# One GpSimd multiplication for keys and receptances, and solve products of the second half in place with 128 columns, in a chunked recurrence with two MLPs

## The chip, the cores and the metric

The kernel runs on one core of one Trainium2 chip. The metric is the device time of one execution in microseconds (us); shorter is better. Engines are called TensorE (PE, with PEld for its weight loads), VectorE (DVE), ScalarE (ACT), GpSimd (POOL) and SyncE (SP). The clock that the profile lists is the one granted to TensorE, as a share of its full speed.

## The reference

For 4 batches and 8 heads, a state of 40 x 40 per head is carried over 768 steps; its outputs then go through two MLPs, token by token.

```
for t in range(S):                      # S = 768, D = 40, B = 4, H = 8
    y[:, :, t] = einsum('bhd,bhde->bhe', r_t, state)
    Sa = einsum('bhde,bhe->bhd', state, a_t)
    state = state * w_t[:, :, None, :] - einsum('bhd,bhe->bhde', Sa, b_t)
    state = state + einsum('bhd,bhe->bhde', v_t, k_t)
x = y by tokens                         # 3072 tokens x 320
h = x @ moe_w_in                        # 320 -> 2048
g = where(h >= 1, h, where(h <= -1, 0, (h + 1) ** 2 / 4))
x = g @ moe_w_out                       # 2048 -> 320
gate = x @ moe2_w_gate ; val = x @ moe2_w_val      # 320 -> 1536 each
out = (silu(gate) * val) @ moe2_w_out   # 1536 -> 320
```

## The kernel before

The sequence is cut into 12 chunks of 64 steps. A chunk of one batch with its 8 heads is a unit, so there are 48 units, numbered chunk by chunk. Within a chunk the recurrence becomes matrix products and one triangular solve; from chunk to chunk only the state is carried. Values that need more than 16 bits are held as a high and a low f16 part, and products are made of the parts.

Work comes in five kinds. `decay_tasks` (three groups of four chunks) multiplies the decays up, on VectorE for the first group and on GpSimd for the others, and writes them to DRAM as `was` and `wks`. `p_tasks` prepares a unit: it loads keys and receptances of two units at a time into the tile `ldp` and multiplies them by the decays. `ldp` has four parts of 128 rows: 0 holds k and b, 1 holds a and r, 2 and 3 hold the decays that they are multiplied by (`wks` in both halves of the rows of part 2, of which the lower is a copy, and `was` in rows 0 to 63 of part 3). In part 1 only a is multiplied by decays (rows 0 to 63, the helper `mul`, L573, on VectorE for chunk 0 and GpSimd for the others); r (rows 64 to 127) is multiplied by 2^8 by the helper `scaled` (L576, GpSimd). Casts on ScalarE (L864, L868) and subtractions (L567) then make the f16 parts, two transposes follow, and products (L885) give the matrices of the unit.

`inv_tasks` inverts the triangular matrices of a chunk's 32 heads, in halves of 32 steps, on VectorE (62 operations in a row, L948 and L953), and stores the result to DRAM, from where `m_tasks` loads it as `tt`. `m_tasks` runs the recurrence of a unit: products into the PSUM tile `px` (L1065), then the solve in two halves of 32 steps. Each half reads its 32 rows of `px`, makes three f16 parts (`xs`) of them, and multiplies by `tt` in 8 products, one per head (`mm_sa`, L1075), that write 32 other rows of `px` (64 to 95, 96 to 127); from these `shi` (L1106) and `slo` make the f16 parts of `vss`. Between the halves 16 products (L1081) subtract the first half from the second. Then follow the products that give the output and the next state (L1142, L1163).

The MLPs run chunk by chunk: `in1` and `in2` with the input products (L1208), `outp` with the output products (L1275), on the PSUM tiles `ph` and `po`. In the beginning PSUM and SBUF lend their tiles to other uses: `po` is at first used for the recurrence of chunk 0 under the name `pq`, and is given to `outp` when the tasks named in `K.grow("po", ...)` have ended. Weights are split into f16 parts by VectorE, ScalarE and GpSimd while the first chunks run.

The order of all instructions on each engine comes from the class `Plan`, which runs at build time. It simulates the engines with the costs given with each task, forward and backward by turns (`rounds`), and emits the tasks in the order of the last forward pass. `lim` bounds how far transfers may queue up ahead, a constant in `forward` and one in `backward` stand for the time to a landing, and the tables `by_chunk` and `by_step` add offsets to the priorities of named tasks: `K.nudge` in every round, `K.last` before the last. A task with `lk=True` may not overlap with one of the other of VectorE and GpSimd in the plan.

Of the kernel before, what the change touches and what calls it, by code (L numbers as in the profile page):

```python
# [15 lines left out]
class Plan:  # L16
# [10 lines left out]
    def __init__(self):  # L27
        self.tasks, self.made, self.pools, self.slots = [], {}, {}, {}
        self.bias, self.unit, self.nudge, self.last = 0.0, ["z", 0, 0], ({}, {}), ({}, {})
        self.lim, self.rounds, self.loose = 1.438, 5, ()  # L30

    def pool(self, name, tiles):
        self.pools[name] = dict(free=list(tiles), users={}, spares=[], grow=[])
# [35 lines left out]
    def forward(self, prio):  # L69
# [59 lines left out]
        while done < len(ts):  # L129
            started = True  # L130
            while started:
                started = False
                for eng in self.ENGINES[:5]:
# [7 lines left out]
                    while any(heaps):  # L141
# [42 lines left out]
                        if t["dma"]:  # L184
                            heapq.heappush(events, (end, -1))
                            dma = max(dma, begin) + t["dma"]
                            end = dma + 1.705
                        else:
                            end += t["lat"]
                        heapq.heappush(events, (end, i))  # L190
# [29 lines left out]
    def backward(self, prio):  # L220
# [14 lines left out]
        now, done, starts, held, events, size = 0.0, 0, [0.0] * len(ts), set(), [], len(ts)  # L235

        def lat(t):
            return 1.13 + t["dma"] if t["dma"] else t["lat"]

        seen = set()  # L240

# [104 lines left out]
def tile_recurrence__then__gated_mlps(  # L346
# [94 lines left out]
    sbt("ldv", [128, 2, H, D], F32, 1)  # L441
    sbt("vh", [128, H, D], F16, 2)
    sbt("xs", [128, H, D], F16, 2)
    sbt("tt", [128, 2, 2, H, HC], F16, 1)
    gfs = sbt("gf", [128, H, C], F32, 1)
    K.pool("sr", [gfs[0][0:D].bitcast(F16).rearrange("p h t -> p (h t)")[:, 0:3 * HD].rearrange(
        "p (l h d) -> p l h d", l=3, h=H)])
# [41 lines left out]
    K.spare("px", ph, first_m)  # L489
    K.pool("pq", po)  # L490
    K.grow("ph", ph, [(("m", n), "sl", 1) for n in range(B)])
    K.grow("po", [po], [(("m", n), x) for n in range(B) for x in ("s2", "xf")])
    late_keys = [("p", n) for n in range(2 * B, NSU)]
    next_keys = [("p", n) for n in range(B, 2 * B)]

# [76 lines left out]
    def mul(e, out, x, y):  # L572
        e.tensor_tensor(out=out, in0=x, in1=y, op=ALU.mult)  # L573

    def scaled(x, scale):
        p_.tensor_scalar(  # L576
            out=x, in0=x, scalar1=scale, scalar2=1.0, op0=ALU.mult, op1=ALU.mult)

    def side(pool, n):

        return (p_, "Pool", c_p(n)) if pool else (v_, "DVE", c_v(n))
# [1 line left out]
    def setup():  # L583
        v_.memset(mask, 2.0**-6)
        for h0 in (0, C):
            p_.affine_select(
                out=mask[h0:h0 + C], in_=mask[h0:h0 + C], pattern=[[1, C]],
                compare_op=ALU.is_gt, fill=0.0, base=0, channel_multiplier=-1,
            )
        p_.memset(eyem, 0.0)  # L590
        for g in range(2):
            p_.affine_select(
                out=eyem[64 * g:64 * g + 64], in_=eyem[64 * g:64 * g + 64],
                pattern=[[-2, 16], [1, HC]], compare_op=ALU.not_equal, fill=1.0, base=-g,
                channel_multiplier=0)
        p_.memset(sel, 0.0)
        for l in range(2):
            p_.affine_select(
                out=sel[:, 0:D], in_=sel[:, 0:D], pattern=[[-1, D]], compare_op=ALU.not_equal,
                fill=2.0**6, base=-D * l, channel_multiplier=1)  # L600
        p_.memset(eye16, 1.0)
        p_.affine_select(
            out=eye16, in_=eye16, pattern=[[1, 128]], compare_op=ALU.is_equal, fill=0.0, base=0,
            channel_multiplier=-1)
        for t in kbs + kbs2 + ars + vss + K.pools["ars"]["spares"][0][0]:
            v_.memset(t[:, :, 120:128], 0.0)
        for t in vss:
            v_.memset(t[64:128, :, 0:120], 0.0)
        v_.memset(ss[0][64:128], 0.0)
        v_.memset(wt[0][:, :, :, 104:128], 0.0)  # L610
        v_.memset(x16[0][:, 704:768], 0.0)

# [209 lines left out]
    def p_tasks(n, p):  # L822
# [24 lines left out]
        if j % 2 == 0:  # L847
# [6 lines left out]
            T(eng, cost, lambda: copy(  # L854
                out=G("ldp", pp)[C:128, 2], in_=G("ldp", pp)[0:C, 2]),
              r=[(pp, 4)], w=[(pp, 2)], use=L, p=p - 4)
            T("Pool", c_ps(2 * HD), lambda: scaled(G("ldp", pp)[C:128, 1], 2.0**8),
              r=[(pp, 1)], w=[(pp, 5)], use=L, p=p - 4)
        e0, eng, cost = side(c in ARP, HD)
        T(eng, cost, lk=True, emit=lambda: mul(e0, f(1)[0:C], f(1)[0:C], f(3)[0:C]),  # L860
          r=[(pp, 1), (pp, 3)] + (["pads"] if c < 2 else []), w=[(key, "ar")], use=L, p=p)
        T("Pool", c_p(HD), lambda: mul(p_, f(0), f(0), f(2)),
          r=[(pp, 0), (pp, 2)], w=[(key, "kb")], use=L, p=p)
        T("ACT", c_s(2 * HD), lambda: s_.activation(  # L864
            out=G("ars", key)[:, :, 0:2 * D].rearrange("p h (x d) -> p h x d", x=2),
            in_=two(f(1)), func=AF.Copy),
          r=[(key, "ar"), (pp, 5)], w=[(key, "arh")], use=L + AS, p=p)
        T("ACT", c_s(2 * HD), lambda: s_.activation(  # L868
            out=hi2(G("kbs", key)), in_=two(f(0)), func=AF.Copy),
          r=[(key, "kb")], w=[(key, "kbh")], use=L + KB_, p=p)  # L870
# [47 lines left out]
    def inv_tasks(c, p):  # L918
# [38 lines left out]
        for i0 in range(0, 2 * HC - 2, span):  # L957
            part = [divmod(i, 2) for i in range(i0, min(i0 + span, 2 * HC - 2))]

            def steps(part=part):  # L960
                for j, q in part:
                    step(j, q)

            T("DVE", sum(c_v((j // 2 + 1) * (HC - 1 - j)) for j, _ in part), steps,
              r=[(key, "j", i0)], w=[(key, "j", min(i0 + span, 2 * HC - 2))], use=ub + pm, p=p)
        T("ACT", c_s(512), lambda: s_.activation(
            out=T16()[:, 0], in_=M(), func=AF.Copy, scale=2.0**8),
          r=[(key, "j", 2 * HC - 2)], w=[(key, "h")], use=ub + pm, p=p)
        T("DVE", c_v(512), lambda: split(T16()[:, 1], M(), 2.0**8, T16()[:, 0]),
          r=[(key, "h")], w=[(key, "l")], use=ub + pm, p=p)  # L970

        for g in range(2):
# [32 lines left out]
    def m_tasks(n, p):  # L1005
# [15 lines left out]
        if j % 2 == 0:  # L1021
# [8 lines left out]
            if not last:  # L1030
# [2 lines left out]
                    in_=fdr[c][ps].unsqueeze(0).to_broadcast([D, 2 * H, D])),  # L1033
                    r=[("f", c)], w=[(mp, "f")], use=FF, p=p + 4, dma=0.36, cost=0.68)
            td = tsd[c][:, :, :, ps]
            DMA(lambda e: e.dma_start(
                out=G("tt", mp)[0:64].rearrange("p f j h t -> p f (j h t)"),
                in_=td.rearrange("l s f b t -> (l s) f (b t)")),
                r=[("tsd", c)], w=[(mp, "tt")], use=TT, p=p - 3, dma=0.5)
            DMA(lambda e: e.dma_start(  # L1040
                out=G("tt", mp)[64:96].rearrange("p f j h t -> p f (j h t)"),
                in_=td[0].rearrange("s f b t -> s f (b t)")),
                r=[("tsd", c)], w=[(mp, "tt")], use=TT, p=p - 3, dma=0.25, cost=0.68)

        T("ACT", c_s(HD), lambda: s_.activation(
# [23 lines left out]
          use=PX + LK + AT + VS + VH, p=p)  # L1069

        def mm_sa(hf):
            sa, tt, xs = hd(G("px", key)), G("tt", mp)[0:96, hf, j % 2], G("xs", (key, hf))[0:96]
            z = 64 + 32 * hf
            for h in range(H):
                t_.matmul(out=sa[z:z + 32, h], lhsT=tt[:, h], rhs=xs[:, h])  # L1075

        def mm_c():
            px, l2, vs = hd(G("px", key)), flat(G("l21", pk)), G("vss", key)
# [11 lines left out]
        def xhi(hf):  # L1090
            px, xs = hd(G("px", key)), G("xs", (key, hf))
            s_.activation(  # L1092
                out=xs[0:32], in_=px[32 * hf:32 * hf + 32], func=AF.Copy, scale=-(2.0**-10))

        def xdup(hf):
            xs = G("xs", (key, hf))
# [1 line left out]

        def xlo(hf):
            xs = G("xs", (key, hf))  # L1100
            split(xs[64:96], hd(G("px", key))[32 * hf:32 * hf + 32], -(2.0**-10),
                  xs[0:32])

        def shi(hf):
            z = slice(64 + 32 * hf, 96 + 32 * hf)
            s_.activation(out=hi2(G("vss", key)[z]), in_=two(hd(G("px", key))[z]),  # L1106
                          func=AF.Copy, scale=2.0**-8)

        def slo(hf):
            z = slice(64 + 32 * hf, 96 + 32 * hf)  # L1110
            vs = G("vss", key)
            split(vs[z, :, D:2 * D], hd(G("px", key))[z], 2.0**-8, vs[z, :, 0:D])

        for hf in range(2):
            T("ACT", c_s(HD), lambda hf=hf: xhi(hf), r=[(key, "x", hf)],
# [2 lines left out]
              w=[(key, "xl", hf)], use=XS[hf], p=p)  # L1118
            T("DVE", c_v(HD), lambda hf=hf: xlo(hf), r=[(key, "xh", hf)], w=[(key, "xl", hf)],
              use=PX + XS[hf], p=p)  # L1120
            T("PE", 0.39, lambda hf=hf: mm_sa(hf), r=[(key, "xl", hf), (mp, "tt")],
              w=[(key, "sa", hf)], use=PX + TT + XS[hf], p=p)
            T("ACT", c_s(2 * HD), lambda hf=hf: shi(hf), r=[(key, "sa", hf)],
              w=[(key, "sh", hf)], use=PX + VS, p=p)
# [190 lines left out]
    def by(tables):  # L1315
        return {(u, i): x for u, table in tables.items() for i, x in table.items()}

    by_chunk = by({
        "m": {40: -5.25},
        "p": {3: 0.02},  # L1320
    })
    by_step = by({
        "d": {84: 0.48},
    })
    K.nudge = by_chunk, by_step
    by_chunk = by({
# [9 lines left out]
    })  # L1336
    by_step = by({
# [10 lines left out]
    })  # L1348
    K.last = by_chunk, by_step

# [142 lines left out]
```

## Time and profile before

| what | us |
|---|---|
| median of 3 runs | 1086.93 |
| lowest, highest run | 1086.08, 1087.52 |
| the profiled execution | 1090.7 |
| its span, first to last instruction | 1089.0 |
| TensorE busy | 897.9 |
| VectorE busy | 761.7 |
| ScalarE busy | 717.1 |
| GpSimd busy | 712.6 |

The busy times are sums over the span and stand for stages with different limits, so the rows further down are taken by stretch. An engine's waits are named by what ended them, which is inferred from semaphores.

### The profile page before, as it was taken

To read this page: it belongs to the slowest core of one execution; us is meant where nothing else is said; L and a number is where in the kernel's file an instruction comes from. 1 tells how busy PE (TensorE), PEld (TensorE's weight loads), DVE (VectorE), ACT (ScalarE), POOL (GpSimd) and SP (SyncE) were. 2 spreads that over 40 slices of the span, in tenths; PEclk is the share of its full clock that TensorE was granted. 3 is DMA by queue.
4 is the path that set the end of the run, shared out by engine and by line. 5 is a ranking of instruction groups with operands and counts; after the bars stand their busy time and mean duration, and the time that the engine had idled before them with its cause. 6 is when DMAs were issued, how large, how long until landed. Compare 5 with 4: busy or idle time off the path is not lost.

```text
span 1089.0 us, 28776 instructions
## 1 busy us (share of the span) xinstructions
PE 897.9 (82%) x10944; PEld 735.4 (68%) x10944; DVE 761.7 (70%) x1874; ACT 717.1 (66%) x1336; POOL 712.6 (65%) x980
## 2 busy tenths in 40 slices
PE   0332336648977999999999989999999999999998
PEld 0221325437755887888888878787888888888887
DVE  8788897898997586795967849657779586441211
ACT  1685676568875967768679767686686774743422
POOL 4479887767886777687688767766857564432222
PEclk9999999869996999999999999999999999999999
DMA  6967798499896798495896865958959443110000
GB/s 222 193 174 186 208 189 206 135 189 214 193 200 153 157 162 144 98 177 132 131 182 113 169 123 117 161 112 141 169 99 164 91 107 68 48 43 20 14 3 26
DMA packets 386195, 147.94 MB, mean 136 GB/s; under 512 B 344536, under 2 KB 362776, under 8 KB 386056
## 3 DMA queue, kind: packets, MB, share of 16 engines
q1 hardware_dynamic: 359717, 131.15, 58.2%
q10 hardware_dynamic: 26339, 14.95, 6.3%
q8 instruction: 86, 1.41, 0.6%
q14 instruction: 53, 0.43, 0.1%
HBM read 78.25 MB, written 21.52 MB: 92 GB/s over the span
## 4 chain that ended last, share of the span: by engine, by line
PE 46%; DVE 15%; ACT 7%; DMA 6%; issue 4%; POOL 3%; SPq 1%; ACTq 0%; DVEq 0%; POOLq 0%
PE ph L1208 24%; PE po L1275 16%; DMA mx<-x 3%; DVE vss L569 2%; PE px L1075 1%; DVE pg L953 1%; PE pg L1163 1%; DVE ub L948 1%; PE px L1065 1%; DMA x2t<-mx 1%; DVE xs L569 1%; DVE px L642 1%; DVE pg L1169 1%; DVE pf L1196 1%; ACT vss L1106 1%
## 5 line engine op out<-in xcount | busy, mean ns | idle before, releaser
L1275 PE MATMUL po<-wo,mx 128*128 128x320 f16 x2016 | 310.7, 301 | 3.8 <-POOL wo L567 1.6
L567 POOL TENSOR_TENSOR mx<-mx 128x512 f16<-128x512 f32 x168 | 194.7, 1162 | 155.9 <-ACT mx L1228 139.4
L1275 PEld LDWEIGHTS <-mx 128*128 128x128 f16 x2016 | 191.2, 98 | 71.8 <-issue 3.6
L1208 PE MATMUL ph<-mx,w 128*128 128x256 f16 x1536 | 198.2, 284 | 18.8 <-DMA mx<-x 12.5
L1208 PEld LDWEIGHTS <-w 128*128 128x128 f16 x1536 | 152.4, 102 | 46.9 <-issue 16.4
L1228 ACT CAST mx<-mx 128x512 f16<-128x512 f32 x168 | 102.4, 614 | 65.3 <-DVE mx L1258 37.2
L1208 PE MATMUL ph<-x2t,wv 128*128 128x256 f16 x1152 | 142.5, 274 | 3.5 <-DVE wv L569 1.5
L1208 PE MATMUL ph<-x2t,wg 128*128 128x256 f16 x1152 | 143.1, 274 | 2.3 <-ACT mx L1255 2.3
L1244 DVE SCALAR_TENSOR_TENSOR mx<-ph,mx 128x512 f32<-128x512 f32 x96 | 66.1, 689 | 98.1 <-ACT mx L1241 97.7
L1208 PEld LDWEIGHTS <-wv 128*128 128x128 f16 x1152 | 110.1, 98 | 17.7 <-DVE wv L569 1.8
L1208 PEld LDWEIGHTS <-wg 128*128 128x128 f16 x1152 | 109.6, 98 | 17.9 <-POOL wg L567 1.5
L953 DVE TENSOR_TENSOR pg<-pg,ub 128x126 f32<-128x126 f32 (+22 forms) x372 | 95.7, 257 | 8.5
L948 DVE SCALAR_TENSOR_TENSOR ub<-ub,pg 128x126 f32<-128x126 f32 (+22 forms) x372 | 91.8, 247 | 11.8 <-DMA ub<-lsd 2.7
L1258 DVE SCALAR_TENSOR_TENSOR mx<-ph,mx 128x512 f32<-128x512 f32 x72 | 49.5, 687 | 69.7 <-PE ph L1208 67.8
L1240 ACT ACTIVATE mx<-ph 128x512 f32<-128x512 f32 x96 | 57.1, 594 | 35.8 <-PE ph L1208 28.7
L573 POOL TENSOR_TENSOR ldp<-ldp 64x320 f32<-64x320 f32 (+1 forms) x90 | 77.0, 865 | 5.0 <-DMA ldp<-was 1.6
L1255 ACT ACTIVATE mx<-ph 128x512 f32<-128x512 f32 x72 | 42.9, 596 | 42.5 <-PE ph L1208 40.8
L1106 ACT ACTIVATE vss<-px 32x640 f16<-32x640 f32 x90 | 61.0, 693 | 12.4 <-PE px L1075 9.3
L1097 POOL COPY xs<-xs 32x320 f16<-32x320 f16 x96 | 42.8, 449 | 39.7 <-ACT xs L1092 34.6
L1241 ACT ACTIVATE mx<-mx 128x512 f32<-128x512 f32 x96 | 60.5, 630 | 3.0
L569 DVE SCALAR_TENSOR_TENSOR vss<-px,vss 32x320 f16<-32x320 f32 x90 | 44.4, 493 | 22.3 <-ACT vss L1106 19.5
L1182 POOL COPY gf<-ss 40x960 f16<-40x960 f16 x44 | 43.5, 990 | 21.2 <-DVE ss L569 10.5
(215 smaller groups left out, 1678.0 us busy)
## 6 DMA issues: line engine op xcount, KB each, us to landing
ldp<-in_kb_dram SPq DMA_DIRECT2D x20, 320.0 KB
ub<-lsd SPq DMA_DIRECT2D x22, 256.0 KB
ldv<-in_v_dram SPq DMA_DIRECT2D x17, 320.0 KB
ldp<-in_ar_dram SPq DMA_DIRECT2D x13, 320.0 KB
wo<-in_wo_dram SPq DMA_DIRECT2D x12, 320.0 KB
out_dram<-mx SPq DMA_DIRECT2D x24, 160.0 KB
waf<-was SPq DMA_DIRECT2D x23, 160.0 KB
wo<-in_w1a_dram SPq DMA_DIRECT2D x7, 512.0 KB
```

Source lines behind the costliest of these rows:

```text
L567: e.tensor_tensor(out=out, in0=x, in1=hi, op=ALU.subtract)
L569: e.scalar_tensor_tensor(out=out, in0=x, scalar=scale, in1=hi, op0=ALU.mult, op1=ALU.subtract)
L573: e.tensor_tensor(out=out, in0=x, in1=y, op=ALU.mult)
L948: v_.scalar_tensor_tensor(out=t, in0=L()[:, j, j + 1:].unsqueeze(1).to_broadcast([128, nm, ni]), scalar=-(2.0**-10), in1=m[:, 0:nm, j:j + ...
L953: v_.tensor_tensor(out=m[:, 0:nm, j + 1:], in0=m[:, 0:nm, j + 1:], in1=t, op=ALU.add)
L1106: s_.activation(out=hi2(G("vss", key)[z]), in_=two(hd(G("px", key))[z]), func=AF.Copy, scale=2.0**-8)
L1208: t_.matmul(out=ps, lhsT=wts[:, wi, fs], rhs=xT[:, xi, :], start=(i == 0), stop=(i == len(plan) - 1))
L1228: T("ACT", c_s(512) - 0.04, lambda: s_.copy(out=G("g", key)[:, 0], in_=u2(key)), r=[(key, "u")], w=[(key, "gh")], use=U + GG, p=p)
L1240: s_.activation(out=u2(key), in_=ps2(key), func=AF.Relu, scale=2.0**-8, bias=1.0)
L1241: s_.activation(out=u2(key), in_=u2(key), func=AF.Square, scale=2.0**3)
L1244: T("DVE", c_v(512, True), lambda: v_.scalar_tensor_tensor(out=u2(key), in0=ps2(key), scalar=2.0**8, in1=u2(key), op0=ALU.max, op1=ALU.min ...
L1275: t_.matmul(out=ps, lhsT=g[:, x, f, 128 * tt:128 * tt + 128], rhs=wo[:, 2 * i + f, y, :], start=(n == 1 and f == 0 and m == 0), stop=(n == ...
```

## The change

Four things are changed. First, rows 64 to 127 of part 3 of `ldp` (both buffers) are set to 2^8 once in `setup`, `scaled` is removed, and part 1 is multiplied by part 3 in all 128 rows. From chunk 1 on, one GpSimd operation multiplies parts 0 and 1 by parts 2 and 3; in chunk 0 there are two operations as before, on VectorE and GpSimd. Second, the solve products add onto the rows of `px` that they are read from (`start=False`) instead of writing rows 64 to 127; for this the inverse's diagonal is set to zero (`strict`) and its sign and scales change. The second half loads 128 columns of `tt`, of which the 32 to 63 are its own, and writes all 128 rows; `tt` is a flat tile with 64 columns of zeros behind. Third, `po` is given to the MLP after the state parts of chunk 0 are made (`"ss"`), not after its scaling (`"s2"`). Fourth, the planner's constants and its tables of offsets are replaced (some 90 entries before, some 600 after; cut here).

```diff
-        self.lim, self.rounds, self.loose = 1.438, 5, ()
+        self.lim, self.rounds, self.loose = 0.73, 2, ()
...
-                            end = dma + 1.705
+                            end = dma + 1.79
...
-            return 1.13 + t["dma"] if t["dma"] else t["lat"]
+            return 1.16 + t["dma"] if t["dma"] else t["lat"]
...
-    sbt("tt", [128, 2, 2, H, HC], F16, 1)
+    tts = sbt("tt", [128, 4 * H * HC + C], F16, 1)
...
-    K.grow("po", [po], [(("m", n), x) for n in range(B) for x in ("s2", "xf")])
+    K.grow("po", [po], [x for n in range(B) for x in (("ss", n), (("m", n), "xf"))])
...
+        for t in [ldp] + K.pools["ldp"]["spares"][0][0]:
+            v_.memset(t[64:128, 3], 2.0**8)
+        v_.memset(tts[0][:, 4 * H * HC:], 0.0)
...
-            T("Pool", c_ps(2 * HD), lambda: scaled(G("ldp", pp)[C:128, 1], 2.0**8),
-              r=[(pp, 1)], w=[(pp, 5)], use=L, p=p - 4)
-        e0, eng, cost = side(c in ARP, HD)
-        T(eng, cost, lk=True, emit=lambda: mul(e0, f(1)[0:C], f(1)[0:C], f(3)[0:C]),
-          r=[(pp, 1), (pp, 3)] + (["pads"] if c < 2 else []), w=[(key, "ar")], use=L, p=p)
-        T("Pool", c_p(HD), lambda: mul(p_, f(0), f(0), f(2)),
-          r=[(pp, 0), (pp, 2)], w=[(key, "kb")], use=L, p=p)
+        if c in ARP:
+            T("Pool", c_p(2 * HD), lambda: mul(
+                p_, G("ldp", pp)[:, 0:2, j % 2], G("ldp", pp)[:, 0:2, j % 2], G("ldp", pp)[:, 2:4, j % 2]),
+              r=[(pp, i) for i in range(4)] + (["pads"] if c < 2 else []), w=[(key, "ar"), (key, "kb")], use=L, p=p)
+        else:
+            T("DVE", c_v(HD), lk=True, emit=lambda: mul(v_, f(1), f(1), f(3)),
+              r=[(pp, 1), (pp, 3)] + (["pads"] if c < 2 else []), w=[(key, "ar")], use=L, p=p)
+            T("Pool", c_p(HD), lambda: mul(p_, f(0), f(0), f(2)),
+              r=[(pp, 0), (pp, 2)], w=[(key, "kb")], use=L, p=p)
...
-          r=[(key, "ar"), (pp, 5)], w=[(key, "arh")], use=L + AS, p=p)
+          r=[(key, "ar")], w=[(key, "arh")], use=L + AS, p=p)
...
+        def strict():
+            for g in range(2):
+                v_.memset(G("pg", key)[64 * g:64 * g + 64, g:g + 15 * (HC + 2) + 1:HC + 2], 0.0)
+
+        T("DVE", 0.17, strict, r=[(key, "j", 2 * HC - 2)], w=[(key, "m")], use=ub + pm, p=p)
...
-            sa, tt, xs = hd(G("px", key)), G("tt", mp)[0:96, hf, j % 2], G("xs", (key, hf))[0:96]
-            z = 64 + 32 * hf
+            sa, tt, xs = hd(G("px", key)), G("tt", mp)[0:96], G("xs", (key, hf))[0:96]
             for h in range(H):
-                t_.matmul(out=sa[z:z + 32, h], lhsT=tt[:, h], rhs=xs[:, h])
+                o = HC * (2 * H * hf + H * (j % 2) + h)
+                out, lhsT = (sa[:, h], tt[:, o - HC:o - HC + 128]) if hf else (sa[0:HC, h], tt[:, o:o + HC])
+                t_.matmul(out=out, lhsT=lhsT, rhs=xs[:, h], start=False, stop=(h == H - 1),
+                          skip_group_check=True)
...
-            T("PE", 0.39, lambda hf=hf: mm_sa(hf), r=[(key, "xl", hf), (mp, "tt")],
+            T("PE", 0.22 if hf else 0.4, lambda hf=hf: mm_sa(hf), r=[(key, "xl", hf), (mp, "tt")],
```

`shi` and `slo` read rows 0 to 63 of `px` instead of 64 to 127, with other scales.

## Rows read from the trace of the kernel before

**Rows 1.** The page: span, busy times, the chain by line.
```profile
span 1089.0 us, 28776 instructions
...
PE 897.9 (82%) x10944; PEld 735.4 (68%) x10944; DVE 761.7 (70%) x1874; ACT 717.1 (66%) x1336; POOL 712.6 (65%) x980
...
PE ph L1208 24%; PE po L1275 16%; DMA mx<-x 3%; DVE vss L569 2%; PE px L1075 1%; DVE pg L953 1%; PE pg L1163 1%; DVE ub L948 1%; PE px L1065 1%; DMA x2t<-mx 1%; DVE xs L569 1%; DVE px L642 1%; DVE pg L1169 1%; DVE pf L1196 1%; ACT vss L1106 1%
```

**Rows 2.** Two stretches: us, busy by engine, granted clock, DMA share, GB/s.
```profile
0.00:354.00 354.00, 180.38 (x2205) 141.21 (x2206) 304.10 (x779) 235.01 (x429) 256.42 (x419) 0.93 0.81 189
354.00:1061.80 707.80, 693.90 (x8544) 574.98 (x8542) 454.81 (x1092) 476.02 (x898) 450.59 (x558) 1.00 0.60 113
```

**Rows 3.** TensorE's waits up to 354 us: total us, times, longest.
```profile
PE ph L1075 <- DMA tt<-tsd: 8.9, 1, 8.9
PE ph L1208 <- DMA mx<-x: 8.0, 2, 6.9
...
PE px L1081 <- POOL vss L1088: 4.8, 1, 4.8
```

**Rows 4.** TensorE's instructions in order of time: start us, us, what.
```profile
360.92 1.04 PE L1208 MATMUL ph<-mx,w 128*128 128x256 f16 x8
361.89 0.57 PE L1075 MATMUL px<-xs,tt 96*32 96x40 f16 x16
362.39 1.05 PE L1208 MATMUL ph<-mx,w 128*128 128x256 f16 x8
363.28 0.40 PE L885 MATMUL pg<-lsp,kbT 120*128 120x64 f16 x8
...
370.25 0.36 PE L1065 MATMUL px<-vh,lkt 128*128 128x40 f16 x8
370.45 0.36 PE L1065 MATMUL px<-vss,lkt 128*128 128x40 f16 x8
...
966.95 0.37 PE L1075 MATMUL px<-xs,tt 96*32 96x40 f16 x8
```

**Rows 5.** VectorE's small memsets of line 996: durations ns min/median/max.
```profile
L996 DVE MEMSET mx<- x24: 85/85/85, 256.4 to 1032.2; 128x32 uint32 x24
```

**Rows 6.** GpSimd: groups of the whole span, then of 0 to 354 us.
```profile
L573 POOL TENSOR_TENSOR ldp<-ldp x90: 849/858/1111, 38.4 to 845.6; 128x320 f32<-128x320 f32 x46, 64x320 f32<-64x320 f32 x44
L573 POOL TENSOR_TENSOR wg<-wg x62: 341/353/643, 45.0 to 127.0; 128x80 f32<-128x80 f32 x62
...
L576 POOL TENSOR_SCALAR ldp<-ldp 64x640 f32<-64x640 f32 x23 | 16.9, 734 | 4.9 <-DMA ldp<-in_ar_dram 3.2
...
L573 POOL TENSOR_TENSOR ldp<-ldp 64x320 f32<-64x320 f32 x16 | 14.0, 879 | 1.0 <-DMA ldp<-was 0.4
L576 POOL TENSOR_SCALAR ldp<-ldp 64x640 f32<-64x640 f32 x9 | 6.5, 723 | 0.8
```

**Rows 7.** VectorE: one multiplication by decays; the splits of the values, early.
```profile
L573 DVE TENSOR_TENSOR mx<-mx x2: 474/809/1144, 39.5 to 42.8; 64x320 f32<-64x320 f32 x2
...
L569 DVE SCALAR_TENSOR_TENSOR vss<-ldv,vh 128x320 f16<-128x320 f32 x15 | 10.8, 720 | 0.2
```

**Rows 8.** GpSimd in order of time, one unit's preparation.
```profile
609.68 0.85 POOL L573 TENSOR_TENSOR ldp<-ldp 64x320 f32<-64x320 f32 x1 [0.18 <-DMA ldp<-was]
...
611.93 0.71 POOL L854 COPY ldp<-ldp 64x640 f32<-64x640 f32 x1 [1.40 <-DMA ldp<-wks]
```

**Rows 9.** VectorE in order of time at the start.
```profile
1.67 1.47 DVE L608 MEMSET vss<- 64x480 uint32 x3
...
5.86 6.24 DVE L573 TENSOR_TENSOR wg<-wg 128x80 f32<-128x80 f32 x16 [1.74 <-DMA wg<-in_w_dram]
```

**Rows 10.** First and last start of the state's cast and of the output products.
```profile
L1172 ACT ACTIVATE ss<-po x4: 685/698/698, 126.6 to 157.2; 40x640 f16<-40x640 f32 x4
...
L1275 PE MATMUL po<-wo,mx x2016: 295/299/475, 179.2 to 1085.1; 128*128 128x320 f16 x184
```

**Rows 11.** Busy time, granted clock and DMA share from 225 to 354 us.
```profile
225.00:354.00 129.00, 99.65 (x1081) 76.18 (x1081) 113.61 (x255) 96.92 (x189) 95.82 (x116) 0.86 0.88 190
```

More of the change, by code (lines that the diff above doesn't have):

```diff
@@ L573, in mul @@
         e.tensor_tensor(out=out, in0=x, in1=y, op=ALU.mult)
-    def scaled(x, scale):
-        p_.tensor_scalar(
-            out=x, in0=x, scalar1=scale, scalar2=1.0, op0=ALU.mult, op1=ALU.mult)
     def side(pool, n):
@@ L965, in inv_tasks @@
               r=[(key, "j", i0)], w=[(key, "j", min(i0 + span, 2 * HC - 2))], use=ub + pm, p=p)
+        def strict():
+            for g in range(2):
+                v_.memset(G("pg", key)[64 * g:64 * g + 64, g:g + 15 * (HC + 2) + 1:HC + 2], 0.0)
+        T("DVE", 0.17, strict, r=[(key, "j", 2 * HC - 2)], w=[(key, "m")], use=ub + pm, p=p)
         T("ACT", c_s(512), lambda: s_.activation(
-            out=T16()[:, 0], in_=M(), func=AF.Copy, scale=2.0**8),
-          r=[(key, "j", 2 * HC - 2)], w=[(key, "h")], use=ub + pm, p=p)
-        T("DVE", c_v(512), lambda: split(T16()[:, 1], M(), 2.0**8, T16()[:, 0]),
+            out=T16()[:, 0], in_=M(), func=AF.Copy, scale=-(2.0**8)),
+          r=[(key, "m")], w=[(key, "h")], use=ub + pm, p=p)
+        T("DVE", c_v(512), lambda: split(T16()[:, 1], M(), -(2.0**8), T16()[:, 0]),
           r=[(key, "h")], w=[(key, "l")], use=ub + pm, p=p)
@@ L1035, in m_tasks, with tiles @@
             td = tsd[c][:, :, :, ps]
+            def tiles(a, b):
+                return G("tt", mp)[a:b, 0:4 * H * HC].rearrange("p (f x) -> p f x", f=2)
             DMA(lambda e: e.dma_start(
-                out=G("tt", mp)[0:64].rearrange("p f j h t -> p f (j h t)"),
-                in_=td.rearrange("l s f b t -> (l s) f (b t)")),
+                out=tiles(0, 64), in_=td.rearrange("l s f b t -> (l s) f (b t)")),
                 r=[("tsd", c)], w=[(mp, "tt")], use=TT, p=p - 3, dma=0.5)
             DMA(lambda e: e.dma_start(
-                out=G("tt", mp)[64:96].rearrange("p f j h t -> p f (j h t)"),
-                in_=td[0].rearrange("s f b t -> s f (b t)")),
+                out=tiles(64, 96), in_=td[0].rearrange("s f b t -> s f (b t)")),
                 r=[("tsd", c)], w=[(mp, "tt")], use=TT, p=p - 3, dma=0.25, cost=0.68)
@@ L1092, in xhi @@
             s_.activation(
-                out=xs[0:32], in_=px[32 * hf:32 * hf + 32], func=AF.Copy, scale=-(2.0**-10))
+                out=xs[0:32], in_=px[32 * hf:32 * hf + 32], func=AF.Copy, scale=-(2.0**-8))
         def xdup(hf):
@@ L1100, in xlo @@
             xs = G("xs", (key, hf))
-            split(xs[64:96], hd(G("px", key))[32 * hf:32 * hf + 32], -(2.0**-10),
+            split(xs[64:96], hd(G("px", key))[32 * hf:32 * hf + 32], -(2.0**-8),
                   xs[0:32])
@@ L1105, in shi @@
             z = slice(64 + 32 * hf, 96 + 32 * hf)
-            s_.activation(out=hi2(G("vss", key)[z]), in_=two(hd(G("px", key))[z]),
-                          func=AF.Copy, scale=2.0**-8)
+            s_.activation(out=hi2(G("vss", key)[z]), in_=two(hd(G("px", key))[32 * hf:32 * hf + 32]),
+                          func=AF.Copy, scale=-(2.0**-10))
         def slo(hf):
@@ L1111, in slo @@
             vs = G("vss", key)
-            split(vs[z, :, D:2 * D], hd(G("px", key))[z], 2.0**-8, vs[z, :, 0:D])
+            split(vs[z, :, D:2 * D], hd(G("px", key))[32 * hf:32 * hf + 32], -(2.0**-10), vs[z, :, 0:D])
         for hf in range(2):
@@ L1318, in tile_recurrence__then__gated_mlps @@
     by_chunk = by({
-        "m": {40: -5.25},
-        "p": {3: 0.02},
[22 rows of a table added]
     })
     by_step = by({
-        "d": {84: 0.48},
[14 rows of a table added]
     })
```

112 rows, old and new, of tables (by_chunk, by_step) are left out of this document.

## The prediction

> **What bounds the kernel now.** I read the page first, then busy time in two stretches, then what TensorE waited for, then single instructions. The page shows a span of 1089.0 us, of which TensorE is busy 897.9 us, more than any other engine, and the chain that ended last is mostly the two groups of MLP products [rows 1]. By stretches there are two stages. Up to 354 us TensorE works 180 of 354 us, VectorE 304 and GpSimd 256; from 354 to 1061.8 us TensorE works 693.9 of 707.8 us and VectorE and GpSimd only about two thirds [rows 2]. The late stage is bound by TensorE: whatever shortens TensorE's own time there shortens the run, and work taken from GpSimd there is hidden. In the early stage TensorE waits for the recurrence, and its longest waits of one piece are DMA landings [rows 3]; VectorE at 86% is the fullest engine.
>
> **Part 1: second-half solve products with 128 columns.** The eight products of one solve half (L1075) load weights of 96x32; the groups that run next to it load 128 columns. Within a run the pace is the same as elsewhere: 16 of them hold 0.50 us (361.89 to 362.39) and 8 products of L1065 hold 0.20 us (370.25 to 370.45), so 25 ns each leaves 0.10 us after the sixteen. Before them the 8 wide products of L1208 take 0.97 us (360.92 to 361.89) against 0.89 us (362.39 to 363.28) when no solve follows: 0.08 to 0.09 us more [rows 4]. One visit to the narrow shape therefore costs about 0.19 us beyond its products, half on entry and half on exit, and this does not depend on whether 8 or 16 products are done in it. The change makes the second half 128 columns wide and leaves the first half at 32. From 361.89 to 966.95 us the trace has 56 visits (the first and the last stand in [rows 4]), 16 of them of sixteen products, that is 72 halves of 36 units (a unit is one chunk of one batch). I take a visit of sixteen to join equal halves of two units, so half the visits, 28, go: 28 x 0.195 = 5.5 us. The bounds are 18 visits (3.5 us, if all paired) and 36 (7.0 us, if none were). All of it lies in the TensorE-bound stage, so it counts in full: **-5.5 us**. In the early stage the visits fall into TensorE's idle time and count nothing; without that cover the 12 early second halves would be at most 12 more, 2.3 us.
>
> The products now add onto the values already in PSUM, which needs the diagonal of the inverse set to zero: two small VectorE memsets per chunk, 24 in all. The nearest memset takes 85 ns [rows 5]: 2 us in all, of which the four chunks inverted early, 8 x 0.085 = 0.7 us, lie on the fullest engine; the later ones are covered by VectorE's idle third. **+0.5 us**, between 0 and 2.
>
> **Part 2: one GpSimd operation for keys and receptances.** It removes the scaling (L576) and, from the second chunk on, merges two multiplications of 0.86 us. The removed scalings are 23 x 0.734 = 16.9 us. The merged form, 128 x 640, is not in the trace. From 353 ns for 80 elements and 858 for 320 per partition the slope is 2.1 ns an element, which gives 858 + 320 x 2.1 = 1.53 us; the bounds are 0.86 us (nothing for the second half) and 1.72 us (two operations). So a merge saves 0.19 us, 44 times: 8 us. GpSimd loses about 25 us of work in total, in the early stage 9 x 0.72 + 16 x 0.19 = 9.5 us [rows 6]. What would that be worth? In the late stage nothing, TensorE covers it. In the early stage TensorE's one long wait for GpSimd there is 4.8 us [rows 3]; so the gain lies between 0 and 4.8 us.
>
> Against it stands what a longer GpSimd operation does to VectorE. The multiplication by decays on VectorE takes 474 ns alone and 1144 ns when GpSimd runs the same kind beside it [rows 7], and the 15 early splits of the values average 720 ns. The difference of the first pair, 0.67 us, is a wait of one for the other. A merged operation of 1.53 us can hold VectorE for 0.67 us longer than one of 0.86 us; if every one of the 16 early ones did, that is 10.7 us. But it also comes once where two came, so most of this cancels. I take gain and loss of GpSimd's part together as **0**, with ends -4.8 and +10.7 us.
>
> The Trainium skill, in "SBUF — State Buffer", section "SBUF: two separate sides", states this as a rule: VectorE operations with two SBUF inputs and GpSimd operations that read SBUF share a port pair, and whichever starts first holds it for its whole instruction. The trace agrees (474 against 1144 ns). By that rule alone, each merge hitting one VectorE operation, the change would be 10.7 us dearer than my sum; it is the fifth case below.
>
> The joint operation also waits for more: the receptances, ready to go when their decays land (609.68), now wait for the key decays and their copy too (611.93 + 0.71) [rows 8], some 3 us later. I cost this at nothing because the first products that use them need the keys as well, and the keys were second before (two operations of 0.86 us, 1.72 us) and are done after 1.53 us now. If something did need the receptances alone, 3 us per chunk would be due in the four early chunks. Queued behind the waiting operation on GpSimd are the low parts of the MLP activations, for which TensorE's output products wait; a merge can hold them up by 0.67 us more, and in the early stage such a hold is part of the +10.7 us above.
>
> **Part 3: the rest.** The constants are written once at the start by VectorE: two memsets of 64 x 640 f32 and a small one. Three of 64 x 480 words take 1.47 us, so these take about 1.4 us, and VectorE then waits 1.74 us for the first decays [rows 9]: covered, cost 0; without that cover 1.4 us. The output banks of the MLP come free after the state's last reader instead of after its scaling. The last such reader starts its wide cast at 157.2 us and one more step follows; the first output product starts at 179.2 us [rows 10]. Cost 0, some 20 us of cover.
>
> **Part 4: the order.** The planner gets another limit for transfers in flight, two rounds instead of five, and other offsets, so every engine's queue is re-sorted. The trace of before cannot show the new order; it shows what is there to win or lose. Between 225 and 354 us TensorE idles 129.0 - 99.65 = 29.3 us, and its granted clock averages 0.86, so 0.14 x 129 = 18 us of full-speed time are lost to stretches at the lower level [rows 11] (these overlap with idling). After 354 another 13.9 us are idle [rows 2]. Single pieces are the waits of 6.9 and 8.9 us [rows 3]. The removed GpSimd work and the smaller limit on transfers both act on that stretch, where DMA is 88% busy. I take one of these waits, the smaller, as gone: **-6.9 us**. The bounds are all 29.3 us gone, and one more wait of the longest kind opened, +8.9 us. This is the weakest term.
>
> **Sum.** -5.5 + 0.5 + 0 + 0 - 6.9 = -11.9 us. The profiled execution took 1090.7 us with a span of 1089.0 us; it becomes about 1077 in span. The median of the runs is 1086.9, 3.8 us below the profiled one, and I apply the difference to it: **1075.0 us**.
>
> **The rivals, with chances.** 0.2% (2.2 us) is about what a measurement of this kernel can tell from no change.
> (1) The sum as above: 1075 us, own range 1064 to 1083. Chance 0.50.
> (2) Only the narrow visits go, and the order neither helps nor hurts: 1086.9 - 5.5 + 0.5 = 1081.9 us. For it: VectorE's early load is not reduced. Chance 0.14.
> (3) The order closes the early hole, 29.3 us: 1086.9 - 5 - 29.3 = 1052.6 us. Against it: VectorE is 88% busy there too (113.6 of 129) [rows 11]. Chance 0.10.
> (4) The late stage is not TensorE's but the recurrence's, which runs through the states from chunk to chunk, so that the 5.5 us turn into idle time: about 1087 us. Against it: only 13.9 of 707.8 us idle. Chance 0.08.
> (5) Slower, by the longer hold on VectorE: 1086.9 - 5 + 10.7 = 1092.6 us. It decides from 8 of the 16 early merges hitting (8 x 0.67 = 5.4 us). Against it: the average early split loses only 720 - 474 = 246 ns to all of GpSimd's work together [rows 7]. Chance 0.08.
> (6) Slower, by the order: a wait of 8.9 us more in the early stage, followed by 10 us at half clock, 5 us: 1086.9 - 5 + 13.9 = 1095.8 us. Chance 0.10.
>
> Faster by over 0.2%: (1), (2) and (3), 0.74; within: 0.08; slower: (5) and (6), 0.18. The range runs from 1056 to 1092: it leaves out half of (3) and most of (6), and the upper part of (5).
>
> **What would show it.** Right: no 96x32 loads in the second half, visits to the narrow shape after the early stage down from 56 to about 28, TensorE's total busy time lower by 3 to 7 us; no L576; 44 GpSimd multiplications of 128 x 640 at about 1.5 us; the late stage still with under 3% idle. The order's term is read from when TensorE becomes full: now about 354 us, by the sum about 347. Wrong: if the wide second half also pauses TensorE on entry; if VectorE's splits beside GpSimd grow well over 720 ns; if TensorE's idle or half-clock time before 360 us grows.

## The result, and the profile after

The changed kernel takes 1077.57 us (median of 5 runs, 1073.86 to 1082.65) against 1086.93 us: ratio 0.9905, 95% interval 0.9877 to 0.9933. Below, a ratio's distance from 1 times 1087 us gives us, so the change is worth 10.3 us (3 us either way; the two medians lie 9.4 us apart). Differences of two ratios carry 3 to 5 us (the root of the sum of the squared half widths). The profiled execution is the slowest of the five, 1082.65 us.

The page of the changed kernel: span, busy times, chain by line.

```profile
span 1080.6 us, 28683 instructions
...
PE 886.9 (82%) x10944; PEld 732.9 (68%) x10944; DVE 760.4 (70%) x1901; ACT 715.4 (66%) x1336; POOL 691.1 (64%) x912
...
PE ph L1218 25%; PE po L1285 15%; DVE ub L949 3%; DVE pg L954 3%; DVE vss L569 3%; PE pg L1173 2%; DMA tt<-tsd 2%; DVE px L641 1%; DMA mx<-x 1%; DVE mx L1254 1%; PE px L1084 1%; DVE px L645 1%; PE px L1073 1%; PE px L1091 1%; DVE xs L569 1%
```

Against [rows 1], TensorE is busy 11 us less and GpSimd 21 us less, and the inverses on VectorE (L949, L954) take 3% each of the chain that ended last instead of 1% each. Its two stretches (columns as in [rows 2]; the last 27.2 us are left off, as there):

```profile
0.00:354.00 354.00, 178.51 (x2228) 142.20 (x2228) 304.21 (x790) 238.55 (x434) 253.33 (x401) 0.88 0.81 191
354.00:1053.40 699.40, 684.53 (x8518) 571.33 (x8518) 453.45 (x1107) 470.32 (x891) 432.01 (x507) 1.00 0.62 114
```

At 354 us the two kernels have done nearly the same number of products (2228 and 2205), so almost all of the 8.4 us between the two profiles is won later, where the stretch is 699.4 us long instead of 707.8. Its idle time is 14.9 us, not less than the 13.9 us of before.

The window from 225 to 354 us (columns as in [rows 11]), and TensorE's waits up to 354 us of the kind of [rows 3]:

```profile
225.00:354.00 129.00, 94.24 (x1084) 74.12 (x1084) 115.26 (x266) 98.28 (x191) 96.33 (x114) 0.87 0.85 193
```
```profile
PE ph L1084 <- DMA tt<-tsd: 11.0, 1, 11.0
PE ph L1218 <- DMA mx<-x: 9.3, 1, 9.3
```

TensorE idles 34.8 us there, where it idled 29.3 us, and both single waits are still there and longer: 11.0 us instead of 8.9, and 9.3 us instead of 6.9.

TensorE in order of time, the same solve as in [rows 4]:

```profile
360.45 0.36 PE L1084 MATMUL px<-xs,tt 96*128 96x40 f16 x8
360.66 1.79 PE L1285 MATMUL po<-wo,mx 128*128 128x320 f16 x12
...
369.13 0.36 PE L1084 MATMUL px<-xs,tt 96*32 96x40 f16 x8 [0.52 <-DMA tt<-tsd]
369.43 0.41 PE L1152 MATMUL pg<-art,vsT 120*128 120x64 f16 x8
```

Eight wide products hold 0.21 us (360.45 to 360.66), eight narrow ones 0.30 us. The pauses of the second half are gone: after 354 us 27 visits to the narrow shape are left of 56.

The other parts: the merged multiplication, the memsets of the diagonal, those of the constants, VectorE's value splits, the first output product (groups by line, then VectorE in order of time).

```profile
L573 POOL TENSOR_TENSOR ldp<-ldp x46: 862/1543/2449, 37.5 to 830.7; 128x640 f32<-128x640 f32 x44, 128x320 f32<-128x320 f32 x2
...
L969 DVE MEMSET pg<- 64x16 f32 x24 | 1.7, 72 | 1.5
...
L569 DVE SCALAR_TENSOR_TENSOR vss<-ldv,vh 128x320 f16<-128x320 f32 x15 | 10.0, 664 | 0.4 <-DMA vsT<-vss 0.3
...
L1285 PE MATMUL po<-wo,mx x2016: 296/299/474, 202.3 to 1076.9; 128*128 128x320 f16 x184
...
3.77 0.59 DVE L607 MEMSET ldp<- 64x640 f32 x1
...
6.38 2.11 DVE L573 TENSOR_TENSOR wv<-wv 128x80 f32<-128x80 f32 x4 [0.87 <-DMA wv<-in_w_dram]
```

The merged operation takes 1.54 us. The early splits average 664 ns, less than the 720 of [rows 7].

### The profile page after: what moved, and what is told of

Its sections match the earlier page's. It is cut to its first block, busy times and chain, and to the rows that moved or that the text cites. A ratio compares the mean times of both kernels' runs of the same rounds, so it can differ in the third digit from the quotient of the medians.

```text
span 1080.6 us, 28683 instructions
## 1 busy us (share of the span) xinstructions
PE 886.9 (82%) x10944; PEld 732.9 (68%) x10944; DVE 760.4 (70%) x1901; ACT 715.4 (66%) x1336; POOL 691.1 (64%) x912
## 4 chain that ended last, share of the span: by engine, by line
PE 47%; DVE 26%; DMA 9%; ACT 6%; issue 5%; POOL 3%; SPq 2%; ACTq 0%; DVEq 0%; POOLq 0%
PE ph L1218 25%; PE po L1285 15%; DVE ub L949 3%; DVE pg L954 3%; DVE vss L569 3%; PE pg L1173 2%; DMA tt<-tsd 2%; DVE px L641 1%; DMA mx<-x 1%; DVE mx L1254 1%; PE px L1084 1%; DVE px L645 1%; PE px L1073 1%; PE px L1091 1%; DVE xs L569 1%
## 5 line engine op out<-in xcount | busy, mean ns | idle before, releaser
L1285 PE MATMUL po<-wo,mx 128*128 128x320 f16 x2016 | 314.5, 304 | 11.1 <-ACT wo L663 5.8
L1218 PE MATMUL ph<-mx,w 128*128 128x256 f16 x1536 | 190.7, 277 | 20.0 <-DMA mx<-x 10.0
L1218 PEld LDWEIGHTS <-w 128*128 128x128 f16 x1536 | 150.0, 99 | 44.7 <-issue 19.5
L1218 PE MATMUL ph<-x2t,wg 128*128 128x256 f16 x1152 | 140.3, 272 | 2.2 <-ACT mx L1265 2.2
L954 DVE TENSOR_TENSOR pg<-pg,ub 128x126 f32<-128x126 f32 (+22 forms) x372 | 95.7, 257 | 8.2
L949 DVE SCALAR_TENSOR_TENSOR ub<-ub,pg 128x126 f32<-128x126 f32 (+22 forms) x372 | 92.0, 247 | 10.9 <-DMA ub<-lsd 1.1
L573 POOL TENSOR_TENSOR ldp<-ldp 128x640 f32<-128x640 f32 (+1 forms) x46 | 70.6, 1545 | 2.6 <-ACT ldp L853 0.6
L1084 PEld LDWEIGHTS <-tt 96*128 96x128 f16 (+1 forms) x768 | 28.1, 96 | 41.4 <-DMA tt<-tsd 15.0
```

The lines of the kernel that those rows point to most:

```text
L949: v_.scalar_tensor_tensor(out=t, in0=L()[:, j, j + 1:].unsqueeze(1).to_broadcast([128, nm, ni]), scalar=-(2.0**-10), in1=m[:, 0:nm, j:j + ...
L954: v_.tensor_tensor(out=m[:, 0:nm, j + 1:], in0=m[:, 0:nm, j + 1:], in1=t, op=ALU.add)
L1218: t_.matmul(out=ps, lhsT=wts[:, wi, fs], rhs=xT[:, xi, :], start=(i == 0), stop=(i == len(plan) - 1))
L1285: t_.matmul(out=ps, lhsT=g[:, x, f, 128 * tt:128 * tt + 128], rhs=wo[:, 2 * i + f, y, :], start=(n == 1 and f == 0 and m == 0), stop=(n == ...
```

## The experiments

The order of all engines is the planner's, and a task that is added or dropped changes it. So each kernel below changes only what a task issues and keeps its cost in the plan: the order stays that of the changed kernel ("new order") or of the kernel before ("old order"). Each was timed in 6 or 12 runs beside the kernel before on the same chip; the chip differs between some of the experiments, so two of them are compared by their ratios.

**narrow_second.**
```diff
-                out, lhsT = (sa[:, h], tt[:, o - HC:o - HC + 128]) if hf else (sa[0:HC, h], tt[:, o:o + HC])
+                out, lhsT = (sa[HC * hf:HC * hf + HC, h], tt[:, o:o + HC])
```


> The changed kernel with the second solve half back at 32 columns, still in place, every engine's order as in the changed kernel. Theory (the pauses of TensorE around the narrow shape count in full in the late stage): 28 visits of 0.195 us come back after 354 us, so 5.5 us slower than the changed kernel, ratio to the kernel before 0.9955 (0.994 to 0.997), TensorE busy about 892 us, late idle unchanged. Rival (the late stage is set by the recurrence's chain and the freed time turned into idle): as fast as the changed kernel, 0.9905.

Measured 1078.64 us, ratio 0.9919 (0.9899 to 0.9939): 1.5 us slower than the changed kernel (4 us either way), not 5.5.

**wide_both.**
```diff
-                out, lhsT = (sa[:, h], tt[:, o - HC:o - HC + 128]) if hf else (sa[0:HC, h], tt[:, o:o + HC])
+                out, lhsT = (sa[:, h], tt[:, o - HC:o - HC + 128]) if hf else (sa[:, h], tt[:, o:o + 128])
```


> The changed kernel with the first solve half at 128 columns as well; its products then also land on the rows of the second half, so the solved values are not the reference's, and the time alone is read. Theory: the remaining 28 visits after 354 us go, 5.5 us faster than the changed kernel, ratio 0.9855 (0.984 to 0.987), no weight load of 32 columns is left. Rival (what is left is bound by the recurrence's chain or by DMA): as fast as the changed kernel, 0.9905.

Measured 1077.64 us, ratio 0.9906 (0.9884 to 0.9928): nothing. Between narrow_second and wide_both all late visits go, 55 of them, which at 0.195 us each are 10.7 us. The late stage of narrow_second, then of wide_both, each from the same product of TensorE's order to the end:

```profile
357.10:1073.30 716.20, 706.65 (x8650) 586.23 (x8646) 452.61 (x1106) 472.03 (x894) 434.41 (x507) 1.00 0.59 110
```
```profile
361.20:1076.30 715.10, 698.35 (x8653) 585.76 (x8648) 452.88 (x1106) 471.18 (x894) 433.43 (x508) 1.00 0.58 111
```

TensorE's own time fell by 8.3 us, and its idle time rose from 9.6 to 16.8 us. These are single executions (that of narrow_second is the fastest of its six), but the ratios say the same: 1.4 us (3 us either way) of the 10.7 arrived. The products became shorter and the end hardly moved.

**less_mlp.**
```diff
-        plan = ((0, 0), (0, 3), (1, 1), (1, 4), (2, 2), (3, 0), (4, 1), (5, 2))
+        plan = ((0, 0), (0, 3), (1, 1), (1, 4), (2, 2), (3, 0), (4, 1))
```


> The changed kernel with one of the eight input products of every MLP step left out (a low part, so the output is less exact): 480 of 3840 products of 0.109 us, 52 us less for TensorE, 45 us of it after 354 us; order as in the changed kernel. Theory of the prediction (the late stage is bound by TensorE): 45 us faster, ratio 0.949. Rival (the late stage is a chain in which TensorE's products, the inverses on VectorE and the loads of their results take turns, so that time freed on TensorE in part turns into waits): 10 to 30 us faster, ratio 0.963 to 0.981.

Measured 1059.28 us, ratio 0.9746 (0.9713 to 0.9779): 17 us faster than the changed kernel, where a stage bound by TensorE would give 45. Its late stretch:

```profile
354.00:1032.70 678.70, 644.99 (x8103) 529.95 (x8104) 451.88 (x1106) 468.36 (x889) 430.38 (x506) 1.00 0.63 117
```

The idle time is 33.7 us instead of 14.9. So about four tenths of what TensorE saves late reach the end (0.3 to 0.5 with the error). A TensorE that is busy 98% of the late stage is not by that its bound: it runs an order fixed in advance, and waits that its own work hides come out when that work shrinks.

**three_ops** (the scaling last in the slot of the merged operation).
```diff
-            T("Pool", c_p(2 * HD), lambda: mul(
-                p_, G("ldp", pp)[:, 0:2, j % 2], G("ldp", pp)[:, 0:2, j % 2], G("ldp", pp)[:, 2:4, j % 2]),
+            def three():
+                mul(p_, f(1)[0:C], f(1)[0:C], f(3)[0:C])
+                mul(p_, f(0), f(0), f(2))
+                if j % 2 == 0:
+                    p_.tensor_scalar(out=G("ldp", pp)[C:128, 1], in0=G("ldp", pp)[C:128, 1],
+                                     scalar1=2.0**8, scalar2=1.0, op0=ALU.mult, op1=ALU.mult)
+            T("Pool", c_p(2 * HD), three,
```


> The changed kernel with the old GpSimd work in the slot of the merged operation: two multiplications per unit and the scaling of 64 x 640 once in two units; every engine's order as in the changed kernel. Theory (GpSimd's work is covered): the same time as the changed kernel within 2 us, ratio 0.989 to 0.992, though GpSimd is busy some 25 us longer. Rival 1 (the freed GpSimd time is what pays): slower by 2 to 5 us, ratio 0.993 to 0.995. Rival 2 (one long operation holds VectorE longer than short ones): faster than the changed kernel by up to 10 us, ratio 0.981 to 0.988.

Measured 1091.55 us, ratio 1.0044 (1.0028 to 1.0061): 15 us slower than the changed kernel. None of the three ranges held it.

**order_alone** (narrow_second and three_ops together).

> Both of the former at once: second half at 32 columns, the old GpSimd operations, in the order of the changed kernel, so that against the kernel before nearly only the order differs (the solve stays in place). Theory (the visits are worth 5.5 us, the rest of the gain of 9.4 us is the order's): ratio 0.9965 (0.995 to 0.998). Rival 1 (the order is the whole gain): 0.9905. Rival 2 (the order gives nothing, the operations everything): 1.000.

Measured 1096.69 us, ratio 1.0086 (1.0068 to 1.0104), outside all three. Either the new order is a bad one that needs the lighter work, or the scaling stood at a bad place in these two kernels.

**two_ops** (the first two lines of `three`, over all 128 rows).
```diff
...
+                mul(p_, f(1), f(1), f(3))
+                mul(p_, f(0), f(0), f(2))
...
```


> The changed kernel with the merged multiplication split in two in its slot (128 x 320 each), without the scaling; order as in the changed kernel. It adds 0.19 us of GpSimd in each of 44 slots, 8 us. The three old operations (25 us more) had cost 14 us, 0.55 us for each us. Theory (GpSimd's time in these slots is on the chain that sets the end): 4.5 us slower than the changed kernel, ratio 0.995 (0.9935 to 0.997). Rival (the scaling, and where it stood in that run, made the loss; the merge itself gives nothing): 0.9905.

Measured 1077.88 us, ratio 0.9909 (0.9884 to 0.9935): the merge itself gives nothing that can be seen (0.4 us, 4 us either way). The scaling, behind the multiplications, made the loss.

**three_early** (the scaling ahead, beside the copy; the multiplications as in three_ops).
```diff
...
+                if c >= NDC:
+                    p_.tensor_scalar(out=G("ldp", pp)[C:128, 1], in0=G("ldp", pp)[C:128, 1],
+                                     scalar1=2.0**8, scalar2=1.0, op0=ALU.mult, op1=ALU.mult)
...
```


> The changed kernel with the old three GpSimd operations again, but the scaling of 64 x 640 beside the copy of the key decays, some microseconds ahead of the multiplications, and no longer behind them in their slot (from the third chunk on; the second chunk keeps the constant). GpSimd does some 23 us more than in the changed kernel, as in the run that lost 14 us. Theory (that loss came from the place: ScalarE's cast of the receptances waited for the scaling, with everything queued behind it): within 2 us of the changed kernel, ratio 0.989 to 0.993. Rival (GpSimd's total work is what counts): 12 us slower than the changed kernel, ratio 1.002.

Measured 1081.67 us, ratio 0.995 (0.9927 to 0.9973): 4.9 us slower than the changed kernel (4 us either way), between theory and rival. Of the 15 us of three_ops, 10 came from the place; the other 5 are the price of GpSimd's work, if the place beside the copy costs nothing, which was not tested.

**three_early_narrow** (narrow_second and three_early together).

> The former with the second solve half at 32 columns too: all work as in the kernel before (the solve in place), in the order of the changed kernel, with no operation at a worse place. Theory (the order is most of the gain, work taken away a quarter): ratio 0.992 to 0.996. Rival 1 (the order gives nothing by itself): 0.999 to 1.002. Rival 2 (the prediction's split, 5.5 us of visits and the rest order): 0.9965.

Measured 1085.13 us, ratio 0.9984 (0.9963 to 1.0005): its interval reaches into rival 1's range and just holds the 0.9965 of rival 2. The new order by itself, with the old work, is worth 1.7 us (2.3 us either way); my theory that it was most of the gain fell. In this order the visits are worth 3.7 us (0.9984 to 0.995) and GpSimd's work 4.9 us (0.995 to 0.9905), each 3 to 4 us either way. Three_early_narrow and three_early differ by 29 late visits; from the same product to the end:

```profile
362.10:1083.00 720.90, 707.45 (x8652) 586.23 (x8648) 451.70 (x1106) 471.77 (x894) 447.37 (x550) 1.00 0.58 110
```
```profile
362.70:1078.10 715.40, 702.31 (x8652) 586.66 (x8648) 451.50 (x1106) 472.14 (x894) 448.00 (x550) 1.00 0.58 111
```

Here TensorE's time falls by 5.1 us, and the whole of it reaches the end in these two executions.

**half_mul.**
```diff
-                p_, G("ldp", pp)[:, 0:2, j % 2], G("ldp", pp)[:, 0:2, j % 2], G("ldp", pp)[:, 2:4, j % 2]),
+                p_, G("ldp", pp)[:, 0:2, j % 2, 0:4], G("ldp", pp)[:, 0:2, j % 2, 0:4], G("ldp", pp)[:, 2:4, j % 2, 0:4]),
```


> The changed kernel with the merged multiplication done for 4 of the 8 heads only (half of the multiplications by decays are left out, so the output is not the reference's). GpSimd loses another 44 x 0.68 = 30 us. Theory in its linear form (0.55 us for each us of GpSimd): 16 us faster than the changed kernel, ratio 0.976. Rival (in the changed kernel GpSimd's slots have become short enough to be off the chain, whose GpSimd share is 3% there against 9% with the old operations): 0.987 to 0.9905.

Measured 1074.48 us, ratio 0.9873 (0.9843 to 0.9902): 3.5 us faster than the changed kernel (4 us either way) for 30 us less of GpSimd. The rival holds: at the changed kernel's load there is little left to win there.

**more_late** (three scalings by 1.0 beside the copy, from the sixth chunk on).
```diff
...
+                for _ in range(3 if c >= 5 else 0):
+                    p_.tensor_scalar(out=G("ldp", pp)[C:128, 1], in0=G("ldp", pp)[C:128, 1],
+                                     scalar1=1.0, scalar2=1.0, op0=ALU.mult, op1=ALU.mult)
...
```


> The changed kernel with three scalings by 1.0 (64 x 640, 0.725 us each) beside the copy of the key decays in the chunks from the sixth on: 14 x 3 x 0.725 = 30 us more of GpSimd, all of it after 354 us; order as in the changed kernel, no value changes. Theory of the prediction (GpSimd's work is covered in the late stage): within 2 us of the changed kernel, ratio 0.989 to 0.993. Rival (GpSimd's work counts in the late stage as it did when 23 us of it, spread over the whole span, cost 4.5 us): 0.2 x 30 = 6 us slower or more, ratio 0.996 and up.

Measured 1090.65 us, ratio 1.0034 (1.0012 to 1.0055): 14 us slower than the changed kernel, for 30 us of GpSimd's work all in the late stage. GpSimd is not covered there. The trace tells where it shows: what ScalarE waited for when it casts the receptances (total us, times, longest), in the changed kernel, three_ops and more_late.

```profile
ACT ars L865 <- POOL ldp L573: 4.5, 5, 1.7
```
```profile
ACT ars L872 <- POOL ldp L861: 10.1, 12, 2.6
```
```profile
ACT ars L871 <- POOL ldp L573: 13.2, 9, 3.6
```

The kernels that lost 14 us and more have ScalarE standing 10 to 13 us before this cast (order_alone 11.0), and behind it in ScalarE's queue stand the MLP's activations and casts. In the changed kernel this wait is 4.5 us, in two_ops, half_mul, three_early and three_early_narrow 1.7, 1.8, 3.6 and 4.0 us. That the large waits and the large losses go together speaks for this path, which is argued and not shown: a kernel that removes the wait and keeps GpSimd's work was not tried. The 4.9 us of three_early it does not explain, since its wait is no longer than the changed kernel's.

**old_order_const.**
```diff
+        for t in [ldp] + K.pools["ldp"]["spares"][0][0]:
+            v_.memset(t[64:128, 3], 2.0**8)
...
-            T("Pool", c_ps(2 * HD), lambda: scaled(G("ldp", pp)[C:128, 1], 2.0**8),
+            T("Pool", c_ps(2 * HD), lambda: None,
...
-        T(eng, cost, lk=True, emit=lambda: mul(e0, f(1)[0:C], f(1)[0:C], f(3)[0:C]),
+        T(eng, cost, lk=True, emit=lambda: mul(e0, f(1), f(1), f(3)),
```


> The kernel before with its own order, but without the scaling: the constant stands beside the decays and the receptance multiplication takes all 128 rows (same length). GpSimd loses 24 x 0.73 = 17.6 us. Theory (GpSimd's time counts whatever the order): 0.55 x 17.6 = 9.6 us faster than before, ratio 0.991. Rival (in the old order the scalings stood in GpSimd's gaps, the loss came from their place in the merged slot): 0.998 to 1.000.

Measured 1087.25 us, ratio 1.0004 (0.9984 to 1.0023): in the old order the 16.5 us by which GpSimd is less busy give nothing.

**old_order_const_wide.**
```diff
...
-                t_.matmul(out=sa[z:z + 32, h], lhsT=tt[:, h], rhs=xs[:, h])
...
+                out, lhsT = (sa[:, h], tt[:, o - 96:o + 32]) if hf else (sa[64:96, h], tt[:, o:o + 32])
+                t_.matmul(out=out, lhsT=lhsT, rhs=xs[:, h])
```


> The former, and the second solve half with 128 columns, its own 32 at the end of the window so that the results land in the same rows as before; order of the kernel before. Theory of the prediction (TensorE's visits count in full in the late stage): 5.5 us faster than the former. Rival (as in the changed kernel, where taking the visits away or bringing them back moved 1 us): within 2 us of the former. Both changes of work without the new order then tell what the merge and the order add up to 0.9905.

Measured 1084.25 us, ratio 0.9979 (0.9952 to 1.0007), 2.7 us less than the former (4 us either way): between theory and rival, and not told apart. The trace has 28 narrow visits after 354 us, half of the 56.

## Why the prediction was right, and where its steps were not

The forecast of 1075.0 us is 2.6 us from the median, and the direction held. Its parts were wrong by more than that and made up for each other, so that the number came so close is luck: nothing was forecast for GpSimd's work and 6.9 us for the order, and the runs give 4.9 and 1.7.

*Part 1, -5.5 us.* The mechanism was right: no pause at the wide second half, 27 visits left after 354 us against the 28 worked out, and TensorE's own time falls by 5.1 us for 29 visits (three_early) and by 8.3 us for 55 (wide_both), where 0.195 us each gives 5.7 and 10.7. The step that failed is "it counts in full", which rested on "the late stage is bound by TensorE". Measured effects of half of the visits are 1.5, 0, 3.7 and 2.7 us, each 3 to 4 us either way; the last two do not exclude 5.5, but all the visits together, from narrow_second to wide_both, give 1.4 us of 10.7. With less_mlp, the late stage passes on four tenths of what TensorE saves, which would be 2 of the 5.5 us. TensorE's total busy time fell by 11 us between the two profiles, more than the 3 to 7 us named as a sign; part of it is clock, since after 354 us the kernel before shows two stretches at the lower level and the changed one shows one. The mechanism of rival (4), not its time, was nearer to this than the sum. The diagonal cost 1.7 us of VectorE in all, within its bounds.

*Part 2, 0.* The length of the merged operation was right (1.53 forecast, 1.54 measured), and so was that the merge as such is worth nothing (two_ops). The step that failed is "in the late stage nothing, TensorE covers it": more_late pays 14 us for 30 us in the late stage alone. GpSimd's old work costs 4.9 us in the new order, which the runs do not split by stage: three_early has done 2212 products by 354 us, the changed kernel 2228, so part of it may lie in the early stage, where the prediction allowed 4.8 us. GpSimd lost 21 us of busy time, not 25. Rival (5), the longer hold on VectorE, did not come: the early splits got shorter, and two_ops against the merged form is 0.4 us. That the receptances wait for the keys costs ScalarE 4.5 us of waiting at most, against 0.6 us in the kernel before.

*Part 3.* The constants' memsets took 1.3 us, as worked out, and were covered: VectorE still waits 0.87 us for its data behind them. The first multiplication by decays starts at 6.38 us instead of 5.86 because its data land later in the new order. The output banks were not needed before 202.3 us, 23 us later than in [rows 10].

*Part 4, -6.9 us.* Mis-sized: the order with the old work is worth 1.7 us (three_early_narrow, and its interval holds zero). The step that failed is to take the smaller of the two early waits as gone: it is 9.3 us long now (6.6 in narrow_second), not 6.9, and TensorE idles 34.8 us from 225 to 354 us, not 29.3. By 354 us it has worked 178.5 us instead of 180.4 and becomes full no sooner. The prediction named growing idle time in this stage as a sign of being wrong, and for this term it was.

So the gain is, in the new order, 1.7 us for the order, 3.7 us for the visits and 4.9 us for GpSimd, 10.3 us together, each of the three 2 to 4 us either way; taken in another sequence the visits give 1.5 and GpSimd 7. In the old order the constant gives nothing and the wide products 2.7 us. The lighter work is thus worth 8.6 us in the new order and 2.3 us, without the merge, in the old one; the difference of 6.3 us is little more than its error of 5 us. It speaks for work and order paying together. Why the old order passes nothing on is open: the merge could not be put into it without changing it, and where GpSimd's slack lies in it was not settled.

## What to carry to other kernels

An engine that is 98% busy in a fixed order is not proven to be the bound: shorten its work by a known amount and see how much arrives at the end; here four tenths did. An engine at two thirds can cost half a microsecond for each one added (14 us for 30 in more_late); the likely path here, another engine's in-order queue behind its result, was not tested. And work is worth what the order lets through: test an operation inside the order that was made for it, and put it where it stood, since the same 0.7 us operation cost about three times as much behind the multiplications (15 us) as ahead of them (5 us).

## What the runs showed of the hardware

A run of products with 32 columns between products with 128 columns costs TensorE 0.09 us on entry and 0.10 us on exit, whether it has 8 or 16 of them; inside, both shapes go at 25 ns each. GpSimd's multiplication takes 858 ns for 128 x 320 and 1543 ns for 128 x 640, and as long on 64 rows as on 128: its time follows the elements of a row.

In the profiled execution of the changed kernel the granted clock averages 0.88 in the first 354 us, against 0.93 before [rows 2]. This is not the order's alone: narrow_second and wide_both, in the same order, show 0.93 and 0.92. All four have done nearly the same number of products by then (2228, 2205, 2252, 2218), so no time of that stage is seen to go with it.

After 354 us the changed kernel has one stretch at the lower of the two levels (0.50, 1.2 GHz) of 3.4 us, and the kernel before two (from 632.3 and 741.5 us). TensorE was at work in it, and had waited 2.57 us just before:

```profile
564.60:568.00 3.40, 3.40 (x19) 2.40 (x17) 0.42 (x1) 1.23 (x2) 0.00 (x0) 0.50 1.08 136
```
```profile
563.58 7.08 PE L1218 MATMUL ph<-mx,w 128*128 128x256 f16 x48 [2.57 <-DMA ldp<-was]
```

At the pace of [rows 4], 0.111 us a product, 48 of them take 5.3 us; here they hold about 7. The two stretches of the kernel before also follow waits, of 2.84 and 2.52 us. Such a wait need not be followed by one: less_mlp waits 2.55 us before 495.8 us and keeps the full clock.

The five runs of the changed kernel spread over 8.8 us, and those of the kernel before beside them over 4.4 us; but beside the experiments the kernel before spreads over 6 to 13 us in 17 to 23 runs, so the change is not seen to make the time less steady. What makes the runs vary stays open.
